# Routed experts' first product by Strassen's seven block products, with TensorE and VectorE in written order and a range check in small pieces

## Chip, cores and metric

The kernel runs on one core of a Trainium2 chip. The metric is the device time of one execution in microseconds (us). The engines are named as the profile names them: PE is TensorE, PEld its weight loads, DVE is VectorE, ACT is ScalarE, POOL is GpSimd, and SP is SyncE, which here only issues transfers.

## What is computed

Three stages in a row, all in 32-bit floating point: an attention scan, a dense mixture, and routed experts. The change concerns the third stage, and the last lines of the second in passing.

```python
def reference(...):
    attn_out = _attn_ref(r, k, v, w, u)          # 2 batches, 8 heads, 768 steps, 48 wide
    x = attn_out as 1536 x 384
    h = x @ w_in                                 # 384 x 2048
    x = (h / (1 + exp(-h))) @ w_out              # 2048 x 384
    P = exp(x @ w_gate - max)                    # 8 experts
    for _ in range(8):
        P /= P.sum(1, keepdims=True) + 1e-09
        P /= P.sum(0, keepdims=True) + 1e-09
        P *= 1536 / 8
    out = 0
    for e in range(8):
        h = maximum(x @ w1[e], 0.0)              # w1[e]: 384 x 1024
        out += P[:, e:e + 1] * (h @ w2[e])       # w2[e]: 1024 x 384
```

## The kernel before

**Products.** Each 32-bit operand is split into a high and a low half of a shorter format (fp32r), and a product is three matmuls: high by high, high by low, low by high. Weights are the stationary operand in a first product, tokens the moving one. "512-wide" says that 512 columns move through TensorE.

**Stages.** The attention scan runs interleaved with the first mixture (`m_l1`, `m_l2`), which works on blocks of 512 or 256 tokens. At its end `logits` and `split_x2` prepare three token blocks of 512 (`tb`), and `sinkhorn` runs its eight rounds while the first expert has begun. Then come 8 experts (`e`) by 3 token blocks by 8 hidden blocks of 128 (`f`), 192 steps.

**A step.** `e_l1` (L662) makes nine 512-wide matmuls (three blocks `d` of the 384 inputs, three matmuls each) into bank 0 or 1 of PSUM; ScalarE takes the relu (L673) into `hh`, and VectorE the low half `hl` (L674). Two steps later `e_l2` (L677) makes twelve 384-wide matmuls into banks 2 to 5, which sum over the hidden blocks; at the last, `f` = 7, the four banks go into `acc`, times the column of `P` (L698, VectorE; ScalarE for the first expert). Three blocks of 512 tokens of the split input lie in `self.x2s`, made by `split_x2` with three casts on ScalarE and three subtractions on VectorE (L628, L629).

**Weights.** They come in pieces of 768 columns, two hidden blocks each: SP issues the load into a raw buffer (two of them, two pieces each), ScalarE casts the high half (L114), GpSimd subtracts for the low half (L115), a few steps ahead of their use (`split_pieces`). Pools of eight tiles hold each kind.

**Range check.** `w_range` (L703) reads `w` and the 64-bit weights of the mixture again, from the expert 4 on, in 3 and 16 pieces through the same raw buffers, and reduces their least and greatest magnitude (L712 and L713; L728 on ScalarE, L729, L731, L732 on VectorE). It decides at the end whether a slower general program has to run.

**Order.** Only the head of the program is written out in order by hand. For the rest a scheduler decides the order on each engine from the order of the calls, the banks and the buffers; an engine then works through its own list in that order and waits where an operand isn't there.

## Time and profile before

| | before |
|---|---|
| time, median of three runs | 1124.72 us (1124.55 to 1126.55) |
| profiled execution: its time | 1124.64 us |
| profiled execution: span of the records | 1122.9 us |
| PE busy | 1104.6 us, 98% of the span, 7376 matmuls |
| PEld busy | 997.1 us, 89% |
| DVE busy | 477.9 us, 43% |
| ACT busy | 322.6 us, 29% |
| POOL busy | 151.0 us, 13% |
| DMA | 71.26 MB, 63 GB/s on average |

The 1.7 us between the span and the profiled execution's own time lie around the records. Weight loads overlap matmuls, so PEld's share adds nothing to PE's. A busy time is an average over stages; what a stage allows is read from that stage. The first mixture and attention end at some 312 us, the experts fill the rest.

### The profile page before, as it was taken

To read this page: it belongs to the slowest core of one execution; us is meant where nothing else is said; L and a number is where in the kernel's file an instruction comes from. 1 tells how busy PE (TensorE), PEld (TensorE's weight loads), DVE (VectorE), ACT (ScalarE), POOL (GpSimd) and SP (SyncE) were. 2 spreads that over 40 slices of the span, in tenths; PEclk is the share of its full clock that TensorE was granted. 3 is DMA by queue.
4 is the path that set the end of the run, shared out by engine and by line. 5 is a ranking of instruction groups with operands and counts; after the bars stand their busy time and mean duration, and the time that the engine had idled before them with its cause. 6 is when DMAs were issued, how large, how long until landed. Compare 5 with 4: busy or idle time off the path is not lost.

```text
span 1122.9 us, 17560 instructions
## 1 busy us (share of the span) xinstructions
PE 1104.6 (98%) x7376; PEld 997.1 (89%) x7376; DVE 477.9 (43%) x873; ACT 322.6 (29%) x615; POOL 151.0 (13%) x127
## 2 busy tenths in 40 slices
PE   8799999999999999999999999999999999999997
PEld 8678899999989999999999999899999989999996
DVE  7999677774434212122222423562364232122221
ACT  3544444345632431122113112321331231111110
POOL 1012011102700130031004002200310130000000
PEclk8899999999999999999999999999999999999999
DMA  6657112200510030011002200530252020000000
GB/s 201 189 177 229 54 59 68 59 16 5 172 55 1 1 89 25 1 49 64 1 1 85 85 1 29 183 118 9 87 185 68 6 80 1 1 1 1 29 29 32
DMA packets 26920, 71.26 MB, mean 63 GB/s; under 512 B 4128, under 2 KB 11280, under 8 KB 26832
## 3 DMA queue, kind: packets, MB, share of 16 engines
q1 hardware_dynamic: 24816, 59.04, 16.8%
q0 software_dynamic: 2016, 11.01, 3.1%
q8 instruction: 60, 0.98, 0.4%
q14 instruction: 28, 0.23, 0.1%
HBM read 65.31 MB, written 2.36 MB: 60 GB/s over the span
## 4 chain that ended last, share of the span: by engine, by line
PE 92%; DVE 3%; DMA 2%; issue 1%; POOL 1%; SPq 0%; ACT 0%; DVEq 0%; ACTq 0%; POOLq 0%
PE bank L685 12%; PE bank L687 11%; PE bank L686 11%; PE bank L669 11%; PE bank L670 11%; PE bank L668 11%; PE bank L593 3%; PE bank L595 3%; PE bank L574 3%; PE bank L594 3%; PE bank L576 3%; PE bank L575 3%; DMA wh<-in_moe_w_in_dram 1%; PE bank L274 1%; PE bank L443 1%
## 5 line engine op out<-in xcount | busy, mean ns | idle before, releaser
L674 DVE SCALAR_TENSOR_TENSOR hl<-bank,hh 128x512 fp32r<-128x512 f32 x192 | 132.2, 690 | 433.7 <-ACT hh L673 433.4
L685 PE MATMUL bank<-whi,hh 128*128 128x384 f32 x768 | 259.2, 338 | 0.7 <-DVE acc L698 0.7
L686 PE MATMUL bank<-wlo,hh 128*128 128x384 f32 x768 | 258.5, 337 | 0.0
L687 PE MATMUL bank<-whi,hl 128*128 128x384 f32 x768 | 254.5, 338 | 0.0
L673 ACT ACTIVATE hh<-bank 128x512 fp32r<-128x512 f32 x192 | 114.4, 597 | 486.4 <-PE bank L670 475.8
L670 PE MATMUL bank<-x2h,wlo 128*128 128x512 f32 x576 | 228.1, 396 | 0.0
L669 PE MATMUL bank<-x2l,whi 128*128 128x512 f32 x576 | 227.6, 395 | 0.0
L668 PE MATMUL bank<-x2h,whi 128*128 128x512 f32 x576 | 224.7, 390 | 0.0
L115 POOL TENSOR_TENSOR wlo<-raw,whi 128x768 fp32r<-128x768 f32 x64 | 117.8, 1852 | 565.1 <-ACT whi L114 547.4
L685 PEld LDWEIGHTS bank<-whi,hh 128*128 128x128 f32 x768 | 144.4, 188 | 9.4 <-ACT wh L728 1.1
L686 PEld LDWEIGHTS bank<-wlo,hh 128*128 128x128 f32 x768 | 144.2, 188 | 7.9 <-issue 0.2
L687 PEld LDWEIGHTS bank<-whi,hl 128*128 128x128 f32 x768 | 144.0, 188 | 2.4
L670 PEld LDWEIGHTS bank<-x2h,wlo 128*128 128x128 f32 x576 | 108.1, 188 | 22.3
L668 PEld LDWEIGHTS bank<-x2h,whi 128*128 128x128 f32 x576 | 108.3, 188 | 17.1 <-issue 0.2
L669 PEld LDWEIGHTS bank<-x2l,whi 128*128 128x128 f32 x576 | 108.1, 188 | 17.1
L114 ACT CAST whi<-raw 128x768 fp32r<-128x768 f32 x64 | 53.3, 836 | 94.6 <-PE bank L669 40.9
L574 PE MATMUL bank<-x1h,whi 128*128 128x256 f32 (+1 forms) x240 | 74.4, 312 | 2.2 <-ACT whi L114 1.8
L593 PE MATMUL bank<-gh,whi 128*128 128x256 f32 (+1 forms) x240 | 74.6, 319 | 1.8 <-ACT gh L581 1.8
L594 PE MATMUL bank<-gl,whi 128*128 128x256 f32 (+1 forms) x240 | 74.0, 309 | 1.0 <-DVE gl L582 1.0
L698 DVE SCALAR_TENSOR_TENSOR acc<-bank,P,acc 128x384 f32<-128x384 f32 x84 | 48.1, 611 | 63.1 <-PE bank L687 63.1
L595 PE MATMUL bank<-gh,wlo 128*128 128x256 f32 (+1 forms) x240 | 73.9, 309 | 0.0
L575 PE MATMUL bank<-x1l,whi 128*128 128x256 f32 (+1 forms) x240 | 73.6, 307 | 0.2 <-DVE x1l L463 0.2
(156 smaller groups left out, 1114.5 us busy)
## 6 DMA issues: line engine op xcount, KB each, us to landing
raw<-in_moe_w_dram SPq DMA_DIRECT2D x64, 384.0 KB, 3.8
wh<-in_moe_w_in_dram SPq DMA_DIRECT2D x8, 768.0 KB, 4.3
wh<-in_moe_w_out_dram SPq DMA_DIRECT2D x8, 768.0 KB, 4.4
at<-in_att_dram SPq DMA_DIRECT2D x12, 484.0 KB, 3.5
raw<-in_moe_w_in_dram POOLq DMA_DIRECT2D x7, 768.0 KB, 4.6
raw<-in_moe_w_out_dram POOLq DMA_DIRECT2D x7, 768.0 KB, 4.5
at<-in_att_dram SPq DMA_DIRECT2D x11, 339.5 KB, 4.1
wt<-in_w_dram SPq DMA_DIRECT2D x3, 768.0 KB, 4.3
```

The source lines that it names most:

```text
L115: (nc.vector if i < N64 else nc.gpsimd).tensor_sub(lo, raw, hi.bitcast(F32))
L574: nc.tensor.matmul(ps, lhsT=wh, rhs=xh[:, d, :], start=(d == 0), stop=False)
L593: nc.tensor.matmul(ps, lhsT=wdh, rhs=gh, start=first, stop=False)
L594: nc.tensor.matmul(ps, lhsT=wdh, rhs=gl, start=False, stop=False)
L668: nc.tensor.matmul(ps, lhsT=wh, rhs=xh[:, d, :], start=(d == 0), stop=False)
L669: nc.tensor.matmul(ps, lhsT=wh, rhs=xl[:, d, :], start=False, stop=False)
L670: nc.tensor.matmul(ps, lhsT=wl, rhs=xh[:, d, :], start=False, stop=(d == 2))
L673: nc.scalar.activation(hh, ps, ACTF.Relu)
L674: nc.vector.scalar_tensor_tensor(hl, ps, 0.0, hh.bitcast(F32), op0=ALU.max, op1=ALU.subtract)
L685: nc.tensor.matmul(ps, lhsT=hh[:, sl], rhs=wh, start=st, stop=False)
L686: nc.tensor.matmul(ps, lhsT=hh[:, sl], rhs=wl, start=False, stop=False)
L687: nc.tensor.matmul(ps, lhsT=hl[:, sl], rhs=wh, start=False, stop=sp)
```

## The change

The first product of the experts is made for a pair of hidden blocks at a time (2p and 2p+1, 96 steps of `e_step` instead of 192 of `e_l1`). Of the three input blocks the first two, with the two hidden blocks and the two halves of the 512 tokens, form a 2x2 by 2x2 block product, for which Strassen's scheme in Winograd's form needs seven block products of 256 tokens instead of eight; the third input block stays as it was, two products of 512. So a step has 6 matmuls of width 512 and 21 of width 256, where two steps of before had 18 of width 512. In exchange there are sums:

- **of the weights:** four blocks s1 to s4, made by `split_pair` on GpSimd from each piece; a tile of high or low halves has nine blocks instead of six.
- **of the tokens:** four blocks t1 to t4 for each `tb`, made by `split_x2` on VectorE.
- **of the products:** the third input block and one product are summed in PSUM by TensorE itself (banks A and B); the others are made in a third bank, C, which is written three times a step, and VectorE (and once ScalarE) collects them in `u` and `su`, and adds these to A and B in place. Relu and low half follow as before.

`e_l2` is called for one of its four banks at a time, between the products of the next step (`fill`). After step 0 TensorE and VectorE run in exactly the order in which the calls are written; the other engines' order is still the scheduler's. The range check runs from the expert 1 on in 57 pieces of 512 columns, one per step, through a buffer of its own; its absolute value becomes a mask on VectorE. The weights of the experts after the first come in another order (four of w2, then four of w1), those of the first mixture lie in tiles of three hidden blocks, the logits use another bank, and `moe2_w1` is laid out on the host in the new block order.

```diff
--- before.py
+++ after.py
...
+            order = [("a", 0), ("b", 0), ("a", 1), ("b", 1), ("a", 2), ("b", 2), ("a", 3), ("b", 3)]
+            for kind, j in order if e == 0 else sorted(order, reverse=True, key=lambda o: (o[0], -o[1])):
...
+                if kind == "a" and u >= 2:
+                    self.split_pair(u - 2, f // 2, raw)
...
+    def w_tiles(self):
+        return tuple(self.wa_p.tile([128, 9 * 128], F32R, tag=n, name="w" + n) for n in ("hi", "lo"))
...
+    def split_pair(self, e, p, raw):
+        nc = self.nc
+        a11, a12, a22, _, _, a21 = (raw[:, j * 128:(j + 1) * 128] for j in range(6))
+        t = self.t_p.tile([128, 512], F32, tag="t", name="ws")
+        s1, s2, s3, s4 = (t[:, j * 128:(j + 1) * 128] for j in range(4))
+        nc.gpsimd.tensor_add(s1, a21, a22)
+        nc.gpsimd.tensor_sub(s3, a11, a21)
+        nc.gpsimd.tensor_sub(s2, s1, a11)
+        nc.gpsimd.tensor_sub(s4, a12, s2)
+        hi, lo = self.wt[e, p, "a"] = self.w_tiles()
+        for src, sl in ((raw[:, 0:640], slice(0, 640)), (t, slice(640, 1152))):
+            nc.scalar.copy(hi[:, sl], src)
+            nc.gpsimd.tensor_sub(lo[:, sl], src, hi[:, sl].bitcast(F32))
...
-        ps = self.bank_y[:, 0:128]
+        ps = self.bank_u[:, 0:128]
...
-        for d in range(3):
-            nc.scalar.copy(hi[:, d, :], self.x2[tb][:, d, :])
-            nc.vector.tensor_sub(lo[:, d, :], self.x2[tb][:, d, :], hi[:, d, :].bitcast(F32))
+        b11, b12, b21, b22 = (x[:, d, o:o + 256] for d in range(2) for o in (0, 256))
+        ta, tb_ = (self.t_p.tile([128, 512], F32, tag="t", name="xt") for _ in range(2))
+        t1, t2, t3, t4 = ta[:, 0:256], ta[:, 256:512], tb_[:, 0:256], tb_[:, 256:512]
+        nc.vector.tensor_sub(t1, b12, b11)
+        nc.vector.tensor_sub(t3, b22, b12)
+        nc.vector.tensor_sub(t2, b22, t1)
+        nc.vector.tensor_sub(t4, b21, t2)
+        for src, j, o in ((b11, 0, 0), (x[:, 1, :], 0, 256), (ta, 0, 768), (t3, 0, 1280), (t4, 1, 0), (x[:, 2, :], 1, 256)):
+            sl = slice(o, o + src.shape[-1])
+            nc.scalar.copy(hl[0][j][:, sl], src)
+            nc.vector.tensor_sub(hl[1][j][:, sl], src, hl[0][j][:, sl].bitcast(F32))
...
-    def e_l1(self, i, e, tb, f):
...
+    def e_banks(self, n):
+        if n < K['ring']:
+            c, a = (7, 0) if n % 2 == 0 else (0, 7)
+            return [self.banks[j] for j in (a, 1, c)]
+        ring = self.ring = [6, 0, 7, 1] if n == K['ring'] else [self.ring[j] for j in (3, 0, 1, 2)]
+        self.bank_w = self.banks[ring[3]]
+        return [self.banks[ring[j]] for j in (1, 2, 0)]
+    def e_step(self, n, e, tb, p, fill, side):
+        nc = self.nc
+        A, Bk, C = self.e_banks(n)
+        X, (wh, wl) = self.x2s[tb], self.wt[e, p, "a"]
+        A0, A1, B0, B1, C0, C1 = (t[:, o:o + 256] for t in (A, Bk, C) for o in (0, 256))
+        W = {k: tuple(t[:, j * 128:(j + 1) * 128] for t in (wh, wl))
+             for j, k in enumerate(("a11", "a12", "a22", "e0", "e1", "s1", "s2", "s3", "s4"))}
+        def mm(ps, w, x, start=False, stop=False):
+            (uh, ul), (xh, xl) = W[w], X[x]
+            nc.tensor.matmul(ps, lhsT=uh, rhs=xh, start=start, stop=False)
+            nc.tensor.matmul(ps, lhsT=uh, rhs=xl, start=False, stop=False)
+            nc.tensor.matmul(ps, lhsT=ul, rhs=xh, start=False, stop=stop)
+        def relu(f, ps, sums):
+            hh = self.h_p.tile([128, 512], F32R, tag="hh", name="hh")
+            hl = self.h_p.tile([128, 512], F32R, tag="hl", name="hl")
+            nc.vector.tensor_add(ps, ps, sums)
+            nc.scalar.activation(hh, ps, ACTF.Relu)
+            self.h[1 + e, tb, f] = (hh, hl)
+            return lambda: nc.vector.scalar_tensor_tensor(hl, ps, 0.0, hh.bitcast(F32), op0=ALU.max, op1=ALU.subtract)
+        u = self.t_p.tile([128, 3, 256], F32, tag="u", name="u", bufs=1)
+        su = self.g_p.tile([128, 2, 256], F32, tag="g", name="su")
+        twice = C0.rearrange("p (o t) -> p o t", o=1).to_broadcast([128, 2, 256])
+        mm(C1, "s1", "t1", start=True, stop=True)
+        mm(C0, "a11", "b11", start=True, stop=True)
+        nc.scalar.copy(u[:, 1], C0)
+        if self.low:
+            self.low()
+        nc.vector.tensor_add(u[:, 2], C1, u[:, 1])
+        side()
+        fill(2)
+        mm(A, "e0", "d2", start=True)
+        mm(A0, "a12", "b21")
+        mm(C0, "s2", "t2", start=True, stop=True)
+        nc.vector.tensor_add(u[:, 0::2], twice, u[:, 1:3])
+        fill(2)
+        mm(A1, "s4", "b22", stop=True)
+        low = relu(2 * p, A, u[:, 1:3].rearrange("p s t -> p (s t)"))
+        mm(Bk, "e1", "d2", start=True)
+        low()
+        fill(1)
+        mm(C0, "s3", "t3", start=True, stop=True)
+        mm(B0, "a22", "t4", stop=True)
+        nc.vector.tensor_add(su, twice, u[:, 0::2])
+        self.low = relu(2 * p + 1, Bk, su.rearrange("p s t -> p (s t)"))
+        fill(8)
...
-        n = NT * DM // (128 * 2 * PIECE)
-        mm = sm.tile([128, 2, n], F32, name="wmm")
-        for i in range(n):
-            t = self.raw_p.tile([128, 2 * PIECE], F32, tag="raw", name="wt")
...
+        n, m = NT * DM // (128 * 512), 2 * PIECE // 512
+        mm = self.ones[:, 8:8 + 2 * (n + m * N64)].rearrange("p (s i) -> p s i", s=2)
+        for i in range(n + m * N64):
+            t = self.t_p.tile([128, 512], F32, tag="w", name="wt", bufs=1)
+            if i < n:
+                nc.sync.dma_start(out=t, in_=self.ins["w"][:, i * 512:(i + 1) * 512])
+            else:
+                j, o = divmod(i - n, m)
+                nc.sync.dma_start(out=t.bitcast(I32), in_=self.pieces[j][3][:, o * 512:(o + 1) * 512])
             yield
+            if i >= n:
+                t = t.rearrange("p (n s) -> p s n", s=2)[:, 1]
+                ti = t.bitcast(I32)
+                nc.vector.tensor_scalar(ti, ti, 0, 0x7FFFFFFF, op0=ALU.logical_shift_left, op1=ALU.bitwise_and)
+                nc.vector.scalar_tensor_tensor(t, t, 0.0, t, op0=ALU.is_equal, op1=ALU.max)
             nc.vector.tensor_reduce(mm[:, 0, i:i + 1], t, axis=AX.X, op=ALU.min)
             nc.vector.tensor_reduce(mm[:, 1, i:i + 1], t, axis=AX.X, op=ALU.max)
...
+            todo = [lambda s=s: self.m_l2(*s[1:]) for s in steps[-2:]]
+            def fill(k):
+                for _ in range(min(k, len(todo))):
+                    todo.pop(0)()
+            split_e = (0, 1, 2, 2, 3, 4, 4, 5, 5, 6, 7, 8)
+            for n, (e, tb, p) in enumerate((e, tb, p) for e in range(E) for tb in range(3) for p in range(4)):
+                if wr is None and not gen and (e, tb) >= K['wr']:
+                    wr = self.w_range()
+                self.e_step(n, e, tb, p, fill, lambda: wr and next(wr, None))
+                if n == 0:
+                    self.low()
+                    self.low = None
+                    self.logits(2)
+                    self.split_x2(2)
+                    self.sinkhorn()
+                    ctx.enter_context(tc.manual_schedule(engines=MANUAL))
+                todo += [lambda e=e, tb=tb, f=f, j=j: self.e_l2(e, tb, f, j) for f in (2 * p, 2 * p + 1) for j in range(4)]
+                self.split_pieces(N64 + 8 * (e + 1) + split_e[n % 12])
+            self.low()
+            fill(8)
...
```

TensorE in the middle of the experts, before: the last three of the nine 512-wide matmuls of a first product into bank 61 (the six ahead of them read the same), and the start of a second product (banks 63 to 66).

```order
L668 MATMUL bank_61<-x2h_3804,whi 128x512
L669 MATMUL bank_61<-x2l_3805,whi 128x512
L670 MATMUL bank_61<-x2h_3804,wlo 128x512
L685 MATMUL bank_63<-whi,hh 128x384
L686 MATMUL bank_63<-wlo,hh 128x384
L687 MATMUL bank_63<-whi,hl 128x384
```

The same place in a step of the changed kernel, from the products of bank A (62) on; bank 68 is C here, in its second use.

```order
L742 MATMUL bank_62<-x2h,whi 128x512
L743 MATMUL bank_62<-x2l,whi 128x512
L744 MATMUL bank_62<-x2h,wlo 128x512
L742 MATMUL bank_62<-x2h,whi 128x256
L743 MATMUL bank_62<-x2l,whi 128x256
L744 MATMUL bank_62<-x2h,wlo 128x256
L742 MATMUL bank_68<-x2h,whi 128x256
L743 MATMUL bank_68<-x2l,whi 128x256
L744 MATMUL bank_68<-x2h,wlo 128x256
L789 MATMUL bank_65<-whi,hh 128x384
```

One third of the 512-wide matmuls of a pair are left, and the 256-wide ones stand between them and the second products; C's first content must have been read before its second is written.

VectorE in two steps with a piece of the range check, before: `hl` and `acc` are the step's own work, `wh` and `whm` the check's.

```order
L674 SCALAR_TENSOR_TENSOR hl<-bank_62,hh 128x512
L729 SCALAR_TENSOR_TENSOR wh_8185<-wh_8185 128x768
L731 TENSOR_REDUCE whm<-wh_8185 128x1
L732 TENSOR_REDUCE whm<-wh_8185 128x1
L674 SCALAR_TENSOR_TENSOR hl<-bank_61,hh 128x512
```

One step of the changed kernel on VectorE, with a piece of the check and the accumulations; `u` and `su` are the sums read from C.

```order
L763 TENSOR_TENSOR u<-bank_68,u 128x256
L825 TENSOR_SCALAR wt<-wt 128x256
L826 SCALAR_TENSOR_TENSOR wt<-wt 128x256
L827 TENSOR_REDUCE ones<-wt 128x1
L828 TENSOR_REDUCE ones<-wt 128x1
L769 TENSOR_TENSOR u<-bank_68,u 128x2x256
L749 TENSOR_TENSOR bank_62<-bank_62,u 128x512
L752 SCALAR_TENSOR_TENSOR hl<-bank_62,hh 128x512
L802 SCALAR_TENSOR_TENSOR acc<-bank_63,P,acc 128x384
L778 TENSOR_TENSOR su<-bank_68,u 128x512
L749 TENSOR_TENSOR bank_67<-bank_67,su 128x512
```

The check's four operations now stand between the step's first sum and its second, L769, and everything that VectorE does for a step stands behind them.

VectorE at the turn from the mixture to the experts, before: `x2l` is the low half of the third token block, `lm` and `mx` begin the sinkhorn rounds.

```order
L605 COPY x_2_3600<-bank_65 128x256
L629 TENSOR_TENSOR x2l_4091<-x_2_3600,x2h_4090 128x512 x3
L674 SCALAR_TENSOR_TENSOR hl<-bank_61,hh 128x512
L674 SCALAR_TENSOR_TENSOR hl<-bank_62,hh 128x512
L620 COPY P<-bank_68 128x4x8
L639 TENSOR_REDUCE lm<-P 128x1
```

The same place in the changed kernel; `xt` are the sums of the tokens.

```order
L681 TENSOR_TENSOR xt<-x_2_3608,xt 128x256
L686 TENSOR_TENSOR x2l<-x_2_3608,x2h 128x512
L749 TENSOR_TENSOR bank_62<-bank_62,su 128x512
L686 TENSOR_TENSOR x2l<-xt,x2h 128x256
L682 TENSOR_TENSOR xt<-x_2_3608,xt 128x256
L763 TENSOR_TENSOR u<-bank_61,u 128x256
L686 TENSOR_TENSOR x2l<-xt,x2h 128x512
L663 COPY P<-bank_67 128x4x8
L752 SCALAR_TENSOR_TENSOR hl<-bank_62,hh 128x512
L686 TENSOR_TENSOR x2l<-x_2_3608,x2h 128x512
L686 TENSOR_TENSOR x2l<-xt,x2h 128x256
L769 TENSOR_TENSOR u<-bank_61,u 128x2x256
```

Ten operations of `split_x2` on VectorE instead of three now stand among those of the first two steps.

## Rows read from the trace of the kernel before

**Rows 1.** The page's head: busy us and share of each engine; the chain by engine.

```profile
PE 1104.6 (98%) x7376; PEld 997.1 (89%) x7376; DVE 477.9 (43%) x873; ACT 322.6 (29%) x615; POOL 151.0 (13%) x127
...
PE 92%; DVE 3%; DMA 2%; issue 1%; POOL 1%; SPq 0%; ACT 0%; DVEq 0%; ACTq 0%; POOLq 0%
```

**Rows 2.** Windows: us, busy us (x) of PE PEld DVE ACT POOL, PEclk, DMA.

```profile
257.00:272.00 15.00, 15.00 (x144) 14.65 (x143) 6.50 (x14) 7.92 (x20) 0.00 (x0) 1.00 0.03 9
272.00:312.00 40.00, 40.00 (x329) 38.10 (x328) 18.44 (x24) 25.80 (x53) 27.68 (x15) 1.00 0.46 138
312.00:370.00 58.00, 58.00 (x312) 51.58 (x311) 22.93 (x60) 13.18 (x23) 1.85 (x1) 1.00 0.05 15
690.00:708.00 18.00, 18.00 (x93) 16.40 (x92) 6.42 (x11) 5.81 (x9) 5.55 (x3) 1.00 0.37 130
```

**Rows 3.** Timeline of PE in the experts: start us, duration us, line, operation.

```profile
701.95 0.33 PE L685 MATMUL bank<-whi,hh 128*128 128x384 f32 x1
...
703.54 0.33 PE L685 MATMUL bank<-whi,hh 128*128 128x384 f32 x1
...
705.44 0.39 PE L668 MATMUL bank<-x2h,whi 128*128 128x512 f32 x1
...
707.52 0.87 PE L687 MATMUL bank<-whi,hl 128*128 128x384 f32 x4
```

**Rows 4.** Timeline of PE late in the first mixture.

```profile
262.00 0.28 PE L574 MATMUL bank<-x1h,whi 128*128 128x256 f32 x1
...
263.20 0.28 PE L575 MATMUL bank<-x1l,whi 128*128 128x256 f32 x1
```

**Rows 5.** Timeline of ACT in the experts; in brackets idle time before and its end.

```profile
664.47 0.60 ACT L673 ACTIVATE hh<-bank 128x512 fp32r<-128x512 f32 x1 [3.59 <-PE bank L670]
...
677.03 0.60 ACT L673 ACTIVATE hh<-bank 128x512 fp32r<-128x512 f32 x1 [3.59 <-PE bank L670]
```

**Rows 6.** Groups by line and form, whole span: busy us, mean ns; last, a clear.

```profile
L674 DVE SCALAR_TENSOR_TENSOR hl<-bank,hh 128x512 fp32r<-128x512 f32 x192 | 132.2, 690 | 433.7 <-ACT hh L673 433.4
L115 POOL TENSOR_TENSOR wlo<-raw,whi 128x768 fp32r<-128x768 f32 x64 | 117.8, 1852 | 565.1 <-ACT whi L114 547.4 <-issue 17.5
L673 ACT ACTIVATE hh<-bank 128x512 fp32r<-128x512 f32 x192 | 114.4, 597 | 486.4 <-PE bank L670 475.8 <-PE bank L686 10.5
L698 DVE SCALAR_TENSOR_TENSOR acc<-bank,P,acc 128x384 f32<-128x384 f32 x84 | 48.1, 611 | 63.1 <-PE bank L687 63.1
...
L731 DVE TENSOR_REDUCE whm<-wh 128x1 f32<-128x768 f32 x16 | 15.2, 947 | 0.2
...
L141 DVE TENSOR_SCALAR cv<-raw 128x768 int32<-128x768 int32 x16 | 8.8, 547 | 0.0
...
L484 DVE MEMSET bank<- x4: 272/298/352, 1.1 to 2.1; 128x288 f32 x2, 128x352 f32 x1, 128x256 f32 x1
```

**Rows 7.** Timeline of one step's end in the experts, then of DVE at accumulations.

```profile
643.11 0.39 PE L670 MATMUL bank<-x2h,wlo 128*128 128x512 f32 x1
...
643.54 0.60 ACT L673 ACTIVATE hh<-bank 128x512 fp32r<-128x512 f32 x1 [2.72 <-PE bank L670]
...
644.17 0.69 DVE L674 SCALAR_TENSOR_TENSOR hl<-bank,hh 128x512 fp32r<-128x512 f32 x1 [2.63 <-ACT hh L673]
...
648.79 0.68 DVE L674 SCALAR_TENSOR_TENSOR hl<-bank,hh 128x512 fp32r<-128x512 f32 x1
649.39 1.13 DVE L698 SCALAR_TENSOR_TENSOR acc<-bank,P,acc 128x384 f32<-128x384 f32 x2
```

**Rows 8.** Groups of DVE from 257 to 272 us, then from 272 to 312.

```profile
L582 DVE TENSOR_TENSOR gl<-g,gh 128x256 fp32r<-128x256 f32 x6 | 2.5, 425 | 7.2 <-ACT gh L581 7.2
...
L582 DVE TENSOR_TENSOR gl<-g,gh 128x256 fp32r<-128x256 f32 x15 | 15.2, 1039 | 12.7 <-ACT gh L581 12.6
```

**Rows 9.** Waits: engine and line, what it waited for, us in total, times, longest.

```profile
ACT whi L114 <- DMA raw<-in_moe_w_dram: 35.6, 15, 5.1
...
DVE cr L656 <- PE bank L655: 15.5, 8, 3.5
```

More of the change, by code (lines that the diff above doesn't have):

```diff
@@ L762, in run @@
             self.sm_p = pool("sm", 1)
-            self.wa_p = pool("wa", 8)
+            self.wa_p = pool("wa", 5)
+            self.wx_p = pool("wx", 1)
             self.wb_p = pool("wb", 8)
@@ new lines, in run @@
+            for i in range(NM):
+                s = steps[i]
+                _, tb, o, n, f = s
+                if tb < 2:
+                    self.split_pieces(int(at(wcurve, i)))
+                for blk in split_at.get(i, ()):
+                    for c in range(3):
+                        self.split_x1(blk, c)
+                self.m_l1(i, tb, o, n, f)
+                if gen and i in x1_at:
+                    self.general_x1(x1_at[i])
+                attn_to(at(curve, i + 1))
+                if tb == 2 and o == 256:
+                    if f == 0:
+                        actx.close()
+                        self.x2s_p = pool("x2s", 1)
+                        self.t_p = pool("t", 2)
+                    if f >= 3 and f % 2 == 1:
+                        self.split_pieces(N64 + f // 2)
+                    if f in (4, 8):
+                        self.split_x2(f // 4 - 1)
+                    if f in (5, 9):
+                        self.logits(f // 4 - 1)
+                if i >= 2:
+                    self.m_l2(*steps[i - 2][1:])
```

196 lines of the change are left out of this document (76 added, 120 removed).

## The prediction, made before the changed kernel ran

> **What bounds the kernel now.** I read the page's head first, then the chain of work that ended last, then busy time by stage. TensorE is busy for 1104.6 of 1122.9 us, and 92% of the chain is TensorE [rows 1]: nearly every microsecond taken from its queue is won, unless a wait takes its place. By stage, from the last stretch of the first mixture on TensorE has no gap, while VectorE works 18.4 of 40 us from 272 to 312 and 22.9 of 58 from 312 to 370 [rows 2]. So the question is twofold: how much TensorE time the block products save, and whether VectorE, which gets the additions, stays out of the way.
>
> What a product costs is the distance between starts, not the printed duration, since products overlap. In the routed experts nine 512-wide ones start within 2.08 us, 0.2311 each, and nine 384-wide within 1.59 us, 0.1767 each [rows 3]. Late in the first mixture ten 256-wide ones take 1.20 us, 0.120 each [rows 4]: four per cent more than half of 0.2311. A pair of hidden blocks takes 18 x 0.2311 + 24 x 0.1767 = 8.40 us; the cadence of the relu, 12.56 us over three blocks, says 8.37 for two [rows 5]. I take 8.37.
>
> **The change, part by part.** First, the products. Per pair, 18 of width 512 become 6 of width 512 and 21 of width 256. Saved: 12 x 0.2311 - 21 x 0.120 = 2.773 - 2.520 = 0.253 us. There are 96 pairs: **24.3 us**. The bound below comes from the spread of the starts: with 0.230 for the 512 it is 23.0. The clock was at its full level (PEclk 1.00) in both stretches [rows 2]. The page "TensorE: Matmul & The Clock Gate" of the Trainium skill, in "Wait — 56ns, not 53.3ns?", gives a warm product its columns at 2.4 GHz plus about 2.5 ns: by it the saving would be an estimated 28.5 us and not 24.3; the 0.120 and 0.2311 measured here decide.
>
> Second, VectorE's step. It now runs in written order, so its chain must fit into TensorE's 8.37 - 0.25 = 8.12 us per pair. I lay it out once. Reading a bank and a tile of 512 takes 0.69, the relu 0.60, a 256-wide two-input operation 0.42 undisturbed [rows 6, 8]. From product to relu and from relu to VectorE some 0.04 each pass, and an operation that waits for nothing can start 0.60 after a 0.69 one began [rows 7]. The chain: sum into bank A 0.73, relu 0.63, low half 0.60, `su` 0.72, sum into bank B 0.73, relu 0.63, low half 0.60, 256-wide addition 0.42, `u` 0.72: 5.8 us. The accumulations, four of about 0.55 in every fourth step, add 1.54 there, since they partly fill the wait for the relu: 0.4 on average. A piece of the range check adds four small operations in 48 steps; from the 768-wide ones (0.55 and 0.95) and the 256-wide 0.42, I put them at 0.28 + 0.42 + 0.39 + 0.39 = 1.5 us. Together 7.7 of 8.12, so it **fits with 0.4 us to spare**. In the step after the accumulations `u` ends at about 5.3 us; the product that overwrites its bank stands at 5.8, so even that step holds. The other 39 steps have 1.9 us to spare.
>
> What before doesn't show is a sum written back into its own bank. Bounds: 0.30, what the 256- to 352-wide clears of a bank take, and the two together, 0.69 + 0.53 for a clear scaled to 512, 1.22 [rows 6]. I take 0.69, the row with the same inputs. At 1.22 the range-check steps would be 0.64 us over TensorE's, 31 us in 48 steps.
>
> Third, GpSimd and ScalarE. Each first-product weight piece adds four 128-wide sums and splits 1152 columns instead of 768. At 1.85 us for 768 [rows 6], 2.4 ns a column, GpSimd goes from 1.85 to about 4.0 us, so 4 x (4.0 + 1.85) = 23 us per expert of 97: not a bound by itself. But it bunches, since weight tiles come free only in the last third of an expert. The casts of those weights stand between two relus in ScalarE's queue and may wait for their load (15 such waits, 35.6 us, before [rows 9]); behind them is the relu, behind that the low half, `u` and the product at 5.8. A relu may be 1.5 us late there before TensorE waits. The range check's loads are small and have a whole step to land; SP queues them behind weight loads that wait for GpSimd. For all of this in the steady part I charge **3 us**, between 0 and the 31 above.
>
> Fourth, the turn from the first mixture to the experts. `split_x2` grows from 6 to 16 operations a block, ten of them on VectorE, all from SBUF to SBUF. Here the profile shows a price: the same 256-wide subtraction took 425 ns while GpSimd was idle (257 to 272) and 1039 ns while it was 69% busy (272 to 312) [rows 2, 8], 0.61 more. The operations that read a bank kept their 0.69. In the order of VectorE, 24 operations lie between `u` of step 0 and `u` of step 1: by the rows 11.9 us of work, and 13 of them take two SBUF inputs, 13 x 0.61 = 7.9 more; with two relu waits 21. TensorE has some 81 x 0.12 + 9 x 0.23 + 6 x 0.18 + 1 = 14 us of work there. So 0 to 7 us of stall, I take 4. Then comes the sinkhorn loop: before, VectorE waited eight times for its product, 15.5 us in all [rows 9], which cost nothing; now, in written order, steps 2 to 6 have 5 x (8.12 - 5.8) = 11.6 us of room for some 13 us of work. Bounds 0 and 16; I take 4. Together **8 us**, between 0 and 23.
>
> The regrouping of the first mixture's weights (three more casts and subtractions), the other logits bank and the reordered tail I cost at nothing: VectorE and ScalarE have half their time free there, and without that cover it is about 2 us. After the last product the same accumulations and stores follow as before.
>
> **Sum.** The profiled execution took 1124.64 us, 1122.9 of them span; the median of the three runs is 1124.72, the same. 1124.64 - 24.3 + 8 + 3 = **1111.3 us**, 1.2% less.
>
> **The rivals.** (a) The gain arrives whole: the turn and the steady part are hidden. 1124.6 - 24.3 + 1 = 1101. For it: the undisturbed sums fit. Against it: 11.9 us of VectorE work beside 14 of TensorE leaves no room for GpSimd's presence.
>
> (b) VectorE becomes the bound in the 48 range-check steps, **slower than before**. Two of the small operations (the mask and the zero test) work on SBUF alone, and both could stretch by 0.61 as the subtraction did. The chain is then 7.7 + 1.2 = 8.9, 0.8 over TensorE's, 38 us in 48 steps: 1111 - 3 + 38 = 1146. If it holds only in the 20 steps with weight splitting, 16 us: 1124. It turns slower than before from 0.34 us over per step. Against it: averaged over an expert GpSimd is busy a quarter of the time, not 69%. The page "SBUF — State Buffer" of the Trainium skill, in "SBUF: two separate sides", says that GpSimd and VectorE hold one pair of ports exclusively for a whole instruction, and that an operation in a two-port mode takes it even with a single input; by it the mask waits too, as I assumed; no row of before shows that for a single input.
>
> (c) The turn costs its upper end, or the steady part 15 us: the gain is eaten and the time is within 0.2% of before, some 1124.
>
> (d) The change does less than it says: 256-wide products between 512- and 384-wide ones start further apart than 0.120. At 0.132 (12 x 0.2311 / 21) nothing is saved and 1124.6 + 11 = 1136 results. Against it: products of different width follow each other at 0.17 to 0.23 in the rows of before without a gap.
>
> **How the numbers follow.** Forecast (1104 to 1120): 0.60. (a) 0.13. (b) 0.13, of which a little ends at no change. (c) 0.08. (d) 0.06. Faster by over 0.2%, below 1122.4, which is about what a measurement can tell from no change: 0.60 + 0.13 and the milder parts of (b) and (c): 0.78. Within 0.2%: 0.08. Slower: 0.14, from (b) and (d). The range runs from 1101, rival (a), to 1127: that leaves out the outer part of (b) and (d) and a little below, under 0.2.
>
> **What would show it.** Right: in the steady steps after the range check, about 8.12 us from one pair to the next and no gap on TensorE; 256-wide products 0.120 apart; a sum into a bank about 0.69; gaps on TensorE in the first six steps, behind VectorE. Wrong: a step of 8.4 or more in the range-check steps with TensorE waiting for `u` (rival b), sums above 0.9, casts on ScalarE that hold the relu for more than 1.5 us, or no gap at the turn (rival a).

## The result, and the profile after

The changed kernel is **slower by 1.1%**: 1138.15 us against 1125.5, a ratio of 1.0106 with a 95% interval of 1.0084 to 1.0129. (The median is of four executions, one of which took 5920.86 us for a reason that no trace shows; the ratio leaves it out, and the other three took 1136.2 to 1139.22.) The prediction was 1111.3 us, with a range of 1101 to 1127. Direction and size were wrong.

The head of the page of the changed kernel, and its chain by engine:

```profile
PE 1093.4 (96%) x8240; PEld 1020.6 (90%) x8240; DVE 816.2 (72%) x1533; ACT 357.7 (31%) x739; POOL 243.5 (21%) x287
...
PE 72%; DVE 21%; ACT 3%; issue 1%; DMA 1%; SPq 0%; DVEq 0%; ACTq 0%
```

Beside [rows 1]: TensorE is busy for 11 us less, but the span is 14.5 us longer, and a fifth of the chain of work that ended last now runs over VectorE. VectorE is still far from full, 72%, so the loss is not an engine at its limit but waits in certain places.

Where they are is read from a cadence. Each step copies its first product out of bank C once (L760 on ScalarE), so the distance between two copies is the length of a step. In the last expert of the changed kernel, timeline of ACT:

```profile
1026.79 0.37 ACT L760 COPY u<-bank 128x256 f32<-128x256 f32 x1
...
1034.83 0.37 ACT L760 COPY u<-bank 128x256 f32<-128x256 f32 x1 [2.92 <-PE bank L744]
...
1043.49 0.37 ACT L760 COPY u<-bank 128x256 f32<-128x256 f32 x1
...
1051.54 0.37 ACT L760 COPY u<-bank 128x256 f32<-128x256 f32 x1
...
1059.60 0.37 ACT L760 COPY u<-bank 128x256 f32<-128x256 f32 x1
```

An undisturbed step takes 8.05 us, less than the 8.12 of the prediction, and 0.32 less than the 8.37 that [rows 5] give for before. One step in four takes 8.66.

The copy misleads where ScalarE casts weights ahead of it: then the copy alone is late. Here are the copies of steps 9 and 10 of expert 5 (9.13 us apart), and TensorE's first product in the same two steps (8.65 apart):

```profile
900.96 0.37 ACT L760 COPY u<-bank 128x256 f32<-128x256 f32 x1 [1.19 <-PE bank L744]
...
910.09 0.37 ACT L760 COPY u<-bank 128x256 f32<-128x256 f32 x1
...
900.01 0.28 PE L742 MATMUL bank<-x2h,whi 128*128 128x256 f32 x1
...
908.66 0.28 PE L742 MATMUL bank<-x2h,whi 128*128 128x256 f32 x1
```

So the table goes by the starts of TensorE's first product in a step (us from one to the next), and so do the experiments below, unless they name the copy:

| place | changed kernel | undisturbed |
|---|---|---|
| experts 1 to 7, step behind VectorE's accumulations (20 of them) | 8.65, also without a range check | 8.05 |
| experts 1 to 4, last two steps | 8.37 to 8.41, 8.79 to 8.82 | 8.05 |
| experts 3 to 5, the first two steps | 8.93 to 9.13, 9.62 (expert 2: 8.29, 8.83) | 8.05, 8.65 (expert 7) |
| end of expert 5, start of 6: end of the range check | 9.88, 8.83 | 8.05 |
| expert 1, the first two steps | 9.09, 9.27 | 8.05 |
| expert 0, step 5 to step 6 to step 7 | 14.92, 9.67 (16.24, 8.26 between the copies) | 8.35, 8.42 (expert 0 of turn, below) |

From the first product of expert 1 to that of the last step TensorE takes 0.3 us less than before (695.9 against 696.1), where 83 x 0.32 = 27 us were to be had. The stretch up to the first product of expert 1 takes 13.5 us more than before, first the kernel before, then the changed one:

```profile
406.83 0.39 PE L668 MATMUL bank<-x2h,whi 128*128 128x512 f32 x1
...
420.31 0.28 PE L742 MATMUL bank<-x2h,whi 128*128 128x256 f32 x1
```

Of these, 3.3 us lie ahead of the 32nd activation of the first mixture (179.51 against 176.26 us), a place that varies: 175.5 to 182.5 us in the fourteen traces with the new first mixture. From the start of the last step (before: of the last pair) to the end it is 1.3 us longer.

### The profile page after: what moved, and what is told of

It is laid out like the page before. It is cut to its first block, busy times and chain, and to the rows that moved or that the text cites. A ratio compares the mean times of both kernels' runs of the same rounds, so it can differ in the third digit from the quotient of the medians.

```text
span 1137.4 us, 20534 instructions
## 1 busy us (share of the span) xinstructions
PE 1093.4 (96%) x8240; PEld 1020.6 (90%) x8240; DVE 816.2 (72%) x1533; ACT 357.7 (31%) x739; POOL 243.5 (21%) x287
## 4 chain that ended last, share of the span: by engine, by line
PE 72%; DVE 21%; ACT 3%; issue 1%; DMA 1%; SPq 0%; DVEq 0%; ACTq 0%
PE bank L790 9%; PE bank L789 9%; PE bank L791 9%; PE bank L742 8%; PE bank L744 8%; PE bank L743 8%; DVE acc L802 4%; DVE hl L752 4%; DVE bank L749 3%; PE bank L636 3%; PE bank L617 3%; PE bank L637 3%; PE bank L638 3%; PE bank L619 3%; PE bank L618 3%; ACT hh L750 2%
## 5 line engine op out<-in xcount | busy, mean ns | idle before, releaser
L742 PE MATMUL bank<-x2h,whi 128*128 128x256 f32 (+1 forms) x864 | 269.3, 312 | 11.3 <-DVE u L763 8.0
L750 ACT ACTIVATE hh<-bank 128x512 fp32r<-128x512 f32 x192 | 115.0, 599 | 514.4 <-DVE bank L749 514.4
L744 PE MATMUL bank<-x2h,wlo 128*128 128x256 f32 (+1 forms) x864 | 265.3, 307 | 0.0
L743 PE MATMUL bank<-x2l,whi 128*128 128x256 f32 (+1 forms) x864 | 264.3, 306 | 0.0
L742 PEld LDWEIGHTS bank<-x2h,whi 128*128 128x128 f32 x864 | 163.0, 189 | 26.3 <-issue 8.0
L744 PEld LDWEIGHTS bank<-x2h,wlo 128*128 128x128 f32 x864 | 162.6, 188 | 8.4
L743 PEld LDWEIGHTS bank<-x2l,whi 128*128 128x128 f32 x864 | 162.8, 188 | 4.4
L188 POOL TENSOR_TENSOR wlo<-raw,whi 128x640 fp32r<-128x640 f32 x32 | 50.5, 1578 | 474.9 <-ACT whi L187 474.8
L749 DVE TENSOR_TENSOR bank<-bank,u 128x512 f32<-128x512 f32 x96 | 67.2, 700 | 51.1 <-PE bank L744 48.2
L769 DVE TENSOR_TENSOR u<-bank,u 128x512 f32<-128x512 f32 x96 | 66.0, 688 | 44.3 <-PE bank L744 44.1
L749 DVE TENSOR_TENSOR bank<-bank,su 128x512 f32<-128x512 f32 x96 | 67.1, 699 | 10.0 <-DVE su L778 0.5
```

Source lines behind the costliest of these rows:

```text
L742: nc.tensor.matmul(ps, lhsT=uh, rhs=xh, start=start, stop=False)
L743: nc.tensor.matmul(ps, lhsT=uh, rhs=xl, start=False, stop=False)
L744: nc.tensor.matmul(ps, lhsT=ul, rhs=xh, start=False, stop=stop)
L749: nc.vector.tensor_add(ps, ps, sums)
L750: nc.scalar.activation(hh, ps, ACTF.Relu)
```

## What the trace says of each place

**Behind the accumulations.** VectorE, then TensorE, in the step of 8.66 us between the copies of 1034.83 and 1043.49:

```profile
1033.86 0.70 DVE L749 TENSOR_TENSOR bank<-bank,su 128x512 f32<-128x512 f32 x1
1034.47 1.66 DVE L802 SCALAR_TENSOR_TENSOR acc<-bank,P,acc 128x384 f32<-128x384 f32 x3
1036.04 0.68 DVE L752 SCALAR_TENSOR_TENSOR hl<-bank,hh 128x512 fp32r<-128x512 f32 x1
1036.64 0.41 DVE L763 TENSOR_TENSOR u<-bank,u 128x256 f32<-128x256 f32 x1
1037.83 0.69 DVE L769 TENSOR_TENSOR u<-bank,u 128x512 f32<-128x512 f32 x1 [0.77 <-PE bank L744]
...
1036.69 0.28 PE L744 MATMUL bank<-x2h,wlo 128*128 128x256 f32 x1
1037.20 0.35 PE L742 MATMUL bank<-x2h,whi 128*128 128x256 f32 x1 [0.23 <-DVE u L763]
```

Three accumulations and the low half stand ahead of `u`, which must have read bank C before TensorE writes it again. By the distance of 0.12 between the products ahead of it TensorE could have started at 1036.81; it starts at 1037.20, when `u` is done. That is 0.47 of the 0.60 us, with the first distance behind the wait (0.19 instead of 0.12). The rest, 0.1, stands ahead of it in the same step, at a product of `e_l2` at 1035.13 that writes the bank which the first of the three accumulations reads until 1035.08.

**Mask and GpSimd.** VectorE and GpSimd in a late step of expert 2, and the same mask (L825) in a step without weight splitting:

```profile
606.30 1.87 POOL L132 TENSOR_TENSOR wlo<-raw,whi 128x768 fp32r<-128x768 f32 x1
...
606.72 1.60 DVE L825 TENSOR_SCALAR wt<-wt 128x256 int32<-128x256 int32 x1
608.35 0.43 DVE L826 SCALAR_TENSOR_TENSOR wt<-wt 128x256 f32<-128x256 f32 x1
...
634.51 0.28 DVE L825 TENSOR_SCALAR wt<-wt 128x256 int32<-128x256 int32 x1
```

0.28 us becomes 1.60, and the mask ends 0.15 after GpSimd's subtraction. Eight of the 48 masks took 1.6 to 1.7 us, and each ended 0.15 after such a subtraction; three zero tests took 1.95 and ended 0.28 after one. All 96 reductions of 256 took 0.41 to 0.42, four of them wholly inside a GpSimd subtraction, and what reads a bank kept its time too: `u` 0.36 to 0.43, the low half 0.64 to 0.69. The page "SBUF — State Buffer" of the Trainium skill, "SBUF: two separate sides", says that GpSimd's instruction and a VectorE operation in a two-port mode, or with two SBUF inputs beside a GpSimd instruction that reads SBUF, lock the shared ports against each other for a whole instruction. The trace agrees in the waits of mask and zero test; in which mode the single-input mask ran, no run here shows.

**The end of the range check.** One matmul writes the range check's result into a bank that the step's low half must have read first:

```profile
919.02 0.19 PE L841 MATMUL bank<-ones,wok 128*1 128x1 f32 x2 [1.44 <-DVE hl L752]
```

GpSimd's instructions are not what it waits for: the two long steps there remain when mask and zero test are left out (mask_out, below).

**The turn.** TensorE and ScalarE around step 6:

```profile
364.33 0.39 PE L715 MATMUL bank<-cs,ones 128*128 128x8 f32 x2 [0.83 <-DVE cs L714]
...
366.58 0.59 PE L715 MATMUL bank<-cs,ones 128*128 128x8 f32 x2 [1.87 <-DVE cs L714]
...
368.99 0.59 PE L715 MATMUL bank<-cs,ones 128*128 128x8 f32 x2 [1.82 <-DVE cs L714]
...
370.22 2.13 ACT L800 ACTIVATE acc<-acc,P 128x384 f32<-128x384 f32 x4 [6.05 <-DVE P L717]
372.26 0.35 ACT L760 COPY u<-bank 128x256 f32<-128x256 f32 x1
```

From step 6 on the products use the bank in which the sinkhorn rounds sum, so the last three rounds stand in a row on TensorE ahead of step 6, and each waits for VectorE's round. ScalarE, too, waits 6.05 us for the finished `P`, ahead of the copy that step 6 needs. Windows show the stretch (columns as in [rows 2]):

```profile
350.00:370.00 20.00, 15.18 (x93) 14.20 (x92) 15.16 (x44) 4.48 (x9) 0.00 (x0) 0.91 0.00 0
364.00:366.00 2.00, 0.39 (x2) 0.30 (x2) 1.86 (x7) 0.17 (x1) 0.00 (x0) 1.00 0.00 0
366.00:368.00 2.00, 0.59 (x2) 0.50 (x2) 1.21 (x5) 0.00 (x0) 0.00 (x0) 0.59 0.00 0
370.00:372.60 2.60, 2.60 (x10) 2.60 (x11) 0.13 (x1) 2.38 (x5) 0.00 (x0) 0.50 0.02 6
```

TensorE stands still for 4.8 us. The granted clock falls to its lower level, 0.50, between 366 and 368 us (the 0.59 of that window puts it at about 366.4), in the second gap and ahead of the third, and is still there from 370 to 372.6, when TensorE is busy again.

## The experiments

Two theories stood against each other from here: **place** (waits, each by what stands ahead of what), and **load** (VectorE has too much to do, and a wait closed at one place opens at the next). All edits are to the changed kernel. The ratio is to the kernel before, on the same chip.

| run | us | ratio, 95% interval |
|---|---|---|
| the change | 1138.15 | 1.0106 (1.0084 to 1.0129) |
| late_acc | 1137.55 | 1.0087 (1.0055 to 1.0118) |
| check_clear | 1125.7 | 0.9983 (0.9967 to 0.9999) |
| turn | 1128.94 | 1.0027 (1.0006 to 1.0048) |
| all_three | 1119.72 | 0.9930 (0.9908 to 0.9953) |
| turn_clear | 1117.64 | 0.9930 (0.9907 to 0.9952) |
| acc_out | 1116.16 | 0.9932 (0.9906 to 0.9959) |
| mask_out | 1128.01 | 1.0019 (1.0005 to 1.0034) |
| acc_split | 1125.18 | 0.9993 (0.9973 to 1.0013) |
| best | 1142.15 | 1.0150 (1.0127 to 1.0172) |
| pe_only | 1138.88 | 1.0114 (1.0085 to 1.0144) |
| sched | 1159.41 | 1.0318 (1.0287 to 1.0349) |
| swap | 1128.69 | 1.0020 (1.0006 to 1.0034) |
| swap_all | 1107.11 | 0.9836 (0.9822 to 0.9849) |

### Range check out of GpSimd's way: check_clear, mask_out

```diff
-lambda: wr and next(wr, None)
+lambda: wr and (e == E - 1 or 1 <= n % 12 <= 8) and next(wr, None)
```

> The changed kernel with the same 57 pieces of the range check, but none in the last three steps and the first of experts 1 to 6, in which GpSimd splits weights; they run on into expert 7, which has none to split. Theory of place: the mask took 1.6 us instead of 0.28 where a GpSimd subtraction was under way, and the steps of 9.13, 8.72 and 8.75 us and those at the border fall to 8.66, 8.05, 8.05 as in expert 6; some 3 us in each of experts 1 to 5, and 2 of the 10.69 at its end: 12 to 15 us, 1123 to 1126. Rival: ScalarE's casts of the weights, which stay, hold the relu; the steps keep their length, and the time stays above 1134.

Measured: 1125.7 us. The last three steps of experts 1 to 5 are 8.65 to 8.67, 8.05, 8.05, and the first two of experts 3 to 6 8.05 and 8.65, as in expert 7. That is 12.2 us less in experts 1 to 7. VectorE's mask in this run, a group by line and form:

```profile
L825 DVE TENSOR_SCALAR wt<-wt 128x256 int32<-128x256 int32 x48 | 13.7, 285 | 0.0
```

In the changed kernel the same row reads 25.6 us, 532 ns. Some 2.6 of the 12.2 us belong to the end of the check, which this run moves too. The rival, ScalarE's casts, costs TensorE nothing in these steps: the relu (L750) comes 0.67 to 0.73 us late behind them in the last three steps of experts 2 to 5, and only the copy, late as well, reads 9.15 (and 7.6 in the next expert's first step, where it catches up). A step grows where a cast has waited for its load: in the first of expert 2 of this run it is 9.47, behind a cast that waited 2.98 us and a relu 2.2 us late.

```diff
-nc.vector.tensor_scalar(ti, ti, 0, 0x7FFFFFFF, op0=ALU.logical_shift_left, op1=ALU.bitwise_and)
-nc.vector.scalar_tensor_tensor(t, t, 0.0, t, op0=ALU.is_equal, op1=ALU.max)
+pass
```

> The changed kernel without the two operations of the range check that write SBUF from SBUF, the mask and the zero test (left out; the two reductions, which read SBUF and write a few numbers, stay). If the loss in the last steps of an expert is the wait of these two for a GpSimd instruction to end, the steps of 9.13, 8.72 and 8.75 us become 8.66, 8.05 and 8.05: 10 to 14 us, 1124 to 1128. If the reductions are held in the same way (0.68 us instead of 0.42 in some places), at most half is won: 1131 to 1134.

(The least magnitude is then compared with -1e30.) Measured: 1128.01, the upper end of what was expected, with 8.65, 8.05 and 8.05 in the last steps of experts 1 to 4; experts 1 to 7 take 8.9 us less. The check stays where it was and its reductions cost TensorE nothing there: it was these two operations. The end of the check stays, with steps of 10.01 and 8.85.

### The turn: turn, turn_clear

```diff
-K = {'ring': 6, ...
+K = {'ring': 8, ...
...
-nc.scalar.activation(acc, acc, ACTF.Copy, scale=g)
+self.scale.append(lambda: nc.scalar.activation(acc, acc, ACTF.Copy, scale=g))
...
+if 9 <= n <= 20:
+    with tc.issue_after(self.copied):      # the step's copy on ScalarE
+        self.scale.pop(0)()
```

> The changed kernel with two edits at the turn: the banks change over at step 8 instead of 6, so that the last three sinkhorn rounds need not stand in a row on TensorE ahead of step 6, and ScalarE multiplies the first expert's sums by P one per step from step 9 on instead of waiting for P 6.05 us ahead of the copy that step 6 needs. Theory: the 16.24 us between steps 5 and 6 falls to 8.3 to 9, and the stretch at half clock behind it goes, 3 us more: 8 to 11 us, 1127 to 1130. Rival: VectorE's sinkhorn work is what is too much for those steps, wherever it is waited for; the 8 us come back as steps of 9 us and more, and under 4 us are won.

Measured: 1128.94. The 16.24 us are 8.27, and no later step of expert 0 is longer than 8.51 (both between the copies). The second step of expert 1 falls from 9.27 to 8.37. The same stretch in this run:

```profile
350.00:370.00 20.00, 20.00 (x132) 19.48 (x131) 15.33 (x39) 5.51 (x12) 0.00 (x0) 1.00 0.00 1
```

VectorE works the same 15 us in it as before the edit, and TensorE does not wait: it was the order, not the sinkhorn work. The two edits were tried together, so what each of them is worth is not shown.

> The changed kernel with the two edits that kept their word together, the turn and the moved range check, without the moved accumulations. They lie in different steps and add: 1138 less 12.5 less 9 = 1116 to 1118. Rival: the accumulations' move was worth something in the three edits together (1119.7); then this is slower than that, 1120 to 1122.

The edit is both of the above. Measured: 1117.64; they add.

### The accumulations: late_acc, all_three, acc_out, acc_split

```diff
+if j < 2: add()
+else: self.late.append(add)      # run behind `u` of the next step
```

> The changed kernel with one move: of the four accumulations that end a token block, the third and fourth stand on VectorE behind `u` of the next step instead of ahead of the low half and `u`. Theory of place: the 8.66 us between the steps with accumulations is 8.05 plus 0.61 of wait for `u`, which stood behind them; it falls to 8.05 to 8.2 in experts 1 to 7, 21 places x 0.5 to 0.6 = 11 to 13 us, so 1125 to 1128. Rival, theory of load: VectorE has too much to do in a step whatever the order; the wait comes back later in the step and the time stays within 4 us of the changed kernel's 1138.

A miss: 1137.55, no gain. Without a check the step falls from 8.65 to 8.5 only, and with one the next step pays, 8.36. VectorE in such a step:

```profile
1038.48 0.61 DVE L807 SCALAR_TENSOR_TENSOR acc<-bank,P,acc 128x384 f32<-128x384 f32 x1
1039.76 0.69 DVE L753 SCALAR_TENSOR_TENSOR hl<-bank,hh 128x512 fp32r<-128x512 f32 x1 [0.66 <-ACT hh L751]
1040.36 0.41 DVE L764 TENSOR_TENSOR u<-bank,u 128x256 f32<-128x256 f32 x1
1040.69 1.13 DVE L807 SCALAR_TENSOR_TENSOR acc<-bank,P,acc 128x384 f32<-128x384 f32 x2
```

The place that two accumulations left is now a wait for the relu, which ScalarE's order has put behind the copy; `u` still stands behind the low half and so behind the relu.

> All three edits together. Theory of place: they add up, as they lie in different steps: 11 to 13, 12 to 15 and 8 to 11 us, so 1099 to 1107, faster than the kernel before by 1.6 to 2.3%. Steps of experts 1 to 7 at 8.05 to 8.2 throughout. Rival, theory of load: closing one wait opens the next, and the sum stays above 1125, no better than the kernel before.

Measured: 1119.72, better than before the change, but the two edits of the turn and the check alone do as well (1117.64; the ratio is 0.9930 in both).

Left out altogether:

```diff
-nc.vector.scalar_tensor_tensor(acc, ps, g, acc, op0=ALU.mult, op1=ALU.add)
+pass
```

> The changed kernel without VectorE's accumulations of experts 1 to 7 (the sums over experts are left out, the products stay). This prices them: if the 0.61 us in each step behind them is all theirs, the steps are 8.05 us, also where the range check runs, and the time is 21 x 0.61 = 13 us shorter, 1124 to 1126. If moving two of them failed since another wait takes over (a copy on ScalarE ahead of the relu, or the check), the steps keep 8.4 us and 4 to 5 us are won, 1133.

The steps that stood behind the accumulations are 8.05, with the check and a weight cast beside them too (8.3 in the second step of experts 2, 4 and 5, where GpSimd splits weights), and experts 1 to 7 take 15.0 us less, near the 13 expected. The time, 1116.16, is lower by more, since the end is shorter too: from the last copy to the end 14 us instead of 20, without four accumulations and with stores that wait for nothing. So the 0.6 is theirs.

```diff
+if j < 2: nc.vector.scalar_tensor_tensor(acc, ps, g, acc, ...)
+else:
+    nc.scalar.activation(t, ps, ACTF.Copy, scale=g)
+    nc.gpsimd.tensor_add(acc, acc, t)
...
+        low()
+        side(1)      # a second piece of the check, in expert 7 alone
```

> The turn and a range check out of the way as before, now with no piece in the step behind the accumulations either (two pieces a step in expert 7), and the accumulations divided: two on VectorE, which fit into its wait for the relu, two on ScalarE (times P) and GpSimd (the sum), behind the copy that the next step needs. If VectorE's order and load in those steps are what is left, all steps of experts 1 to 7 are 8.05 to 8.15 us: 1117 less 21 x 0.55 = 1104 to 1107. If ScalarE's or GpSimd's part holds TensorE instead, the steps stay at 8.5 and more: 1116 or above.

(The run also queues ScalarE's copy behind the relu.) Half of it came: experts 2 to 6 take 97.0 to 97.1 us (99 to 102 in the change), which is 8.09 a step. Expert 7, with two pieces of the check in each step, takes steps of 8.8 to 10.0 us behind its first, 102.5 for the 11 distances that take 90.4 in the change. There the theory of load holds: a piece is 1.44 us on VectorE (from the mask at 634.51 to the next sum at 635.95 in the changed kernel), and an undisturbed step has no room for two. Expert 0 takes 135.0 us, 3 more than in turn_clear; why is open.

### A combination that failed: best

```diff
+with self.tc.issue_after(self.relued):      # ScalarE's weight casts and copy behind the relu
...
+e == E - 1 or n % 12 in (range(10) if e == 1 else range(1, 9))      # one piece a step
```

> The changed kernel with the turn's two edits, the accumulations divided between VectorE and ScalarE with GpSimd, ScalarE's copy and weight casts queued behind the relu that VectorE waits for, and the 57 pieces of the range check one per step, the 9 without a mask in expert 1, the others in steps 1 to 8 of experts 2 to 6 and in expert 7. If the three waits found (accumulations ahead of `u`, mask behind GpSimd, relu behind a cast) are all there is in experts 1 to 7, their steps are 8.05 to 8.1 us, 97 us an expert also in the last, and 1117.6 less 13 gives 1103 to 1106: faster than the kernel before by 1.9 to 2.1%. If something else in the accumulating steps or the check's last steps is left, 8.3 to 8.5 us in every fourth, it stays above 1109.

A miss by 38 us: 1142.15. Behind the relu, the casts came in other steps, so GpSimd's subtractions (one at 533.16 us, in the third step of expert 2), and its new sums, now run beside the check. Its mask and zero test in this run:

```profile
L844 DVE TENSOR_SCALAR wt<-wt 128x256 int32<-128x256 int32 x48 | 43.6, 908 | 0.0
...
L845 DVE SCALAR_TENSOR_TENSOR wt<-wt 128x256 f32<-128x256 f32 x48 | 34.6, 721 | 1.7
```

908 ns against 532 in the change and 285 in check_clear. Expert 1, whose pieces have no mask here, takes 97.2 us; experts 2 to 6 102.8 to 103.4. It is the wait for GpSimd once more, from the other side; expert 0, 136.4 us against 131.7 in turn_clear, adds some 5.

### Who writes the order: pe_only, sched

```diff
-MANUAL = {mybir.EngineType.PE, mybir.EngineType.DVE}
+MANUAL = {mybir.EngineType.PE}
```

> The changed kernel with only TensorE in written order; VectorE's order is the scheduler's again, which puts `u` ahead of the low half in the steps behind the accumulations, and spreads the range check over the step. If it is the written order on VectorE that costs the 0.61 us behind the accumulations, they shrink, and with the last steps of the experts unchanged it is 1122 to 1132. If the scheduler's order holds TensorE elsewhere (a low half, which the second products need, behind the check), the steps grow: above 1138.

1138.88, neither. The scheduler hurries the masks: they run from the end of expert 0 to the third step of expert 3, and experts 0 to 2 take 150, 107 and 104 us (140, 101 and 100 in the change). Behind them, experts 4 and 7 have no step above 8.06, the ones behind the accumulations included (the end of the check still lengthens the border of experts 5 and 6). VectorE in expert 7:

```profile
1041.79 0.61 DVE L802 SCALAR_TENSOR_TENSOR acc<-bank,P,acc 128x384 f32<-128x384 f32 x1
1042.32 0.41 DVE L763 TENSOR_TENSOR u<-bank,u 128x256 f32<-128x256 f32 x1
1042.65 0.68 DVE L752 SCALAR_TENSOR_TENSOR hl<-bank,hh 128x512 fp32r<-128x512 f32 x1
```

It has put `u` ahead of the low half, and of the last three accumulations two ahead of the sum into the bank. That points at the written order; the first of the two is tried below.

> The changed kernel without any written order: both engines as the scheduler puts them. It prices the part of the change that writes the order. If the written order brings what it is written for, this is slower than the changed kernel's 1138 by 5 us or more. If the written order is the fault, it is faster, below 1130.

1159.41. The loss lies in experts 0 to 2 (153, 109 and 115 us, with the check in a hurry; 140, 101 and 100 in the change); experts 4 to 6 take 96.6 to 96.9 (99 to 102). So the written order pays in the first experts and costs in the later ones.

### One exchange: swap, swap_all

```diff
-        if self.low:
-            self.low()
         nc.vector.tensor_add(u[:, 2], C1, u[:, 1])
+        if self.low:
+            self.low()
```

> The changed kernel with two neighbours on VectorE exchanged in every step: `u`, which frees the bank that TensorE writes next, stands ahead of the low half, which TensorE needs only 3 us later. If the 0.61 us behind the accumulations and the 0.47 us behind a weight cast are waits for `u` alone, both go: 21 x 0.61 + 5 x 0.47 = 15 us, 1122 to 1125; the last steps of experts 1 to 5 keep the mask's wait, 8.7 us. If VectorE is full in those steps, since accumulations and check together fill it, the steps with a check keep 8.4 us and more, and 1131 or above results.

Measured: 1128.69, 9.5 us less, outside what was expected. The steps behind the accumulations fall from 8.65 to 8.2 or 8.3, with a check or without, so VectorE was not full; 0.15 to 0.2 stays. The 0.47 of the casts was none of TensorE's to win. The last two steps of experts 2 to 4 and the first behind them take 26.5 to 26.6 us together (26.2 to 26.3 in the change): the zero test, later now, meets GpSimd and takes 1.95.

> The exchange together with the turn's two edits and the moved range check. If the three causes are complete, the steps of experts 1 to 7 are 8.05 to 8.1 us, and 1117.6 less 14 gives 1102 to 1106, faster than the kernel before by 1.7 to 2.1%. If the check's pieces in the accumulating steps hold TensorE, as they did with GpSimd's sums beside them, it is 1110 or more.

Measured: **1107.11 us**, faster than the kernel before by 1.64% (1.51 to 1.78%). Experts 1 to 6 take 97.1 to 97.3 us. The head of its page, its chain, and the place that was 8.66:

```profile
PE 1078.8 (98%) x8240; PEld 1015.6 (92%) x8240; DVE 798.5 (72%) x1533; ACT 354.4 (32%) x739; POOL 242.4 (22%) x287
...
PE 90%; DVE 5%; DMA 2%; ACT 1%; issue 1%; SPq 1%; POOL 0%; DVEq 0%; ACTq 0%
```

```profile
1001.43 1.66 DVE L803 SCALAR_TENSOR_TENSOR acc<-bank,P,acc 128x384 f32<-128x384 f32 x3
1003.01 0.42 DVE L762 TENSOR_TENSOR u<-bank,u 128x256 f32<-128x256 f32 x1
1003.34 0.68 DVE L753 SCALAR_TENSOR_TENSOR hl<-bank,hh 128x512 fp32r<-128x512 f32 x1
```

What remains of the wait there, 0.15 to 0.2 us, stands at the bank of the first of the three accumulations, which ends at 1002.04 (1001.43 and 0.61): TensorE's next product into it starts at 1002.10, and the one behind it 0.28 instead of 0.17 later. In acc_out, without accumulations, the step is 8.05.

```profile
1001.90 0.33 PE L792 MATMUL bank<-whi,hl 128*128 128x384 f32 x1
1002.10 0.44 PE L790 MATMUL bank<-whi,hh 128*128 128x384 f32 x1
1002.38 0.34 PE L791 MATMUL bank<-wlo,hh 128*128 128x384 f32 x1
```

VectorE is as busy as in the changed kernel, 72%, and 90% of the chain is TensorE's again. Most of the gain was there, 19.5 us against before on the same chip of the 30.7 that the products save; places in the order had eaten it.

## Why the prediction was wrong, step by step

**The products: right, and a little small.** 0.253 us a step were forecast, 0.32 measured (8.37 less 8.05), 30.7 us in 96 steps instead of 24.3. The 256-wide products start 0.118 apart, not 0.120. The estimate by the page "TensorE: Matmul & The Clock Gate" of the Trainium skill, "Wait — 56ns, not 53.3ns?", 28.5, lies nearer than mine, though in the sum alone: its starts, by estimate 0.216 us for 512 columns and 0.109 for 256, are both below the 0.231 and 0.118 of the traces. Rival (d) fell.

**Durations on VectorE: right.** A sum into its own bank takes 0.70 us where 0.69 was taken between 0.30 and 1.22. Page of the changed kernel, groups by line and form:

```profile
L749 DVE TENSOR_TENSOR bank<-bank,u 128x512 f32<-128x512 f32 x96 | 67.2, 700 | 51.1 <-PE bank L744 48.2
...
L778 DVE TENSOR_TENSOR su<-bank,u 128x512 f32<-128x512 f32 x96 | 65.3, 680 | 0.0
...
L763 DVE TENSOR_TENSOR u<-bank,u 128x256 f32<-128x256 f32 x96 | 39.7, 413 | 2.7 <-ACT u L760 2.5
...
L825 DVE TENSOR_SCALAR wt<-wt 128x256 int32<-128x256 int32 x48 | 25.6, 532 | 0.0
```

**"In the step after the accumulations `u` ends at about 5.3 us; the product that overwrites its bank stands at 5.8, so even that step holds": the step that failed first.** From the sum into bank A (1030.58) `u` ended at 6.47 us, and the product could have started at 6.23. In a step without accumulations `u` ends at 5.2 and the product starts at 6.1. The prediction's own terms would have said so: its chain up to the end of `u` adds up to 5.06, and 1.54 for the accumulations makes it 6.6, not 5.3. Price: 20 x 0.60 = 12 us, where the whole steady part was put at 3.

**"0.61 more" for the mask and the zero test (rival b): right mechanism, wrong size, wrong chance.** The wait is not a stretch of 0.61 but lasts until GpSimd's instruction ends, up to 1.5 us. It lengthened some 16 steps, all among those with weight splitting, the rival's milder form, for which 16 us were worked out; by the table it costs 10.7. I gave it no share in the forecast, by GpSimd's average of a quarter; but what counts is whether it works in the step in which the mask comes.

**The end of the range check: no term.** 2.6 us, for a matmul that waits for a bank.

**"A relu may be 1.5 us late there before TensorE waits": too much.** From the 5.2 and 6.1 above it is 0.9. A relu 0.73 us late cost nothing (check_clear); in the changed kernel one 1.98 late, behind a cast that had waited 2.59 for its load, cost 1.0 in the first step of expert 1. In the second, ScalarE's accumulations of the first expert stand ahead of the relu: 1.2 us, of which 0.9 went in turn.

**The turn: 8 us forecast, some 14 measured** (13.5 us more than before, plus the 12 x 0.32 that the block products save there, less the 3.3 at the head). What I counted, VectorE's work in the first steps (steps of 8.3 to 9.3 us between the copies), was about right; missing were the bank that changes hands at step 6, which puts three rounds in a row, ScalarE's wait for `P`, and the half clock. The turn's two edits won 9 us.

**Sum.** 1124.6 less 30.7, less 1.4 of uneven steps that the kernel before has in experts 4 to 6, and 12 (accumulations) + 10.7 (mask) + 2.6 (end of the check) + 2.3 (first two steps of expert 1) + 14 (turn) + 3.3 (head) + 1.6 (tail, with the 0.3 that its pair saves), some 46, is 1139, the profiled execution's 1139.22. The prediction had 11 for these 46; its rival (c) had a steady part of 15 at most, where the first four terms make 27.6. With the accumulations, the mask, the end of the check and the turn mended, swap_all stands at 1107; that it is near the 1111 forecast says nothing for the forecast, which was of another kernel.

Still open: the head of the program, which in fourteen traces of the same first mixture ends anywhere between 0.8 us earlier and 6.3 later than in the one trace of before, and the longer tail.

## What to carry to other kernels

A fixed order is judged by its tightest place, not by the sum of work in a step: for each step that differs (an accumulation, a cast, a border) note when the next writer wants the bank back and what stands ahead of its last reader. Put the operation that frees a resource ahead of the one that is only needed later. Small operations of VectorE of the two kinds that waited here, mask and zero test from SBUF to SBUF, belong in steps in which GpSimd is idle, or not on the path; what they cost is the rest of GpSimd's instruction, not a percentage. And read a cadence on the engine whose time counts: the copy on ScalarE showed 0.47 us in five steps that TensorE never lost.
